# Attention, a dense FFN and routed experts in one kernel: scores and values as two operations of the first stage's plan

## The chip, the cores and the metric

The kernel runs on one core of a Trainium2 chip. The metric is the device time of one execution in microseconds; the kernel before was timed in three runs, and the median counts. The engines have queues of their own and wait for one another through semaphores: TensorE (PE: matmuls; PEld: its weight loads), VectorE (DVE), ScalarE (ACT), GpSimd (POOL) and SyncE (SP). In this kernel SP issues nearly all loads and POOL the stores to scratch memory.

## The reference

Three layers, one behind the other, on 4 batches of 448 tokens (1792 rows of 768):

```python
scores = scale * np.matmul(q, k.transpose(0, 1, 3, 2)) - np.log(S)   # q, k, v: 4 x 12 heads x 448 x 64, f32
attn = 1.0 / (1.0 + np.exp(-scores))                                  # a sigmoid, not a softmax
x = np.matmul(attn, v)                                                # heads are then joined: 1792 x 768
h = x @ w_in                                                          # 768 x 2048, float64 in memory
x = np.maximum(0.01 * h, h) @ w_out                                   # 2048 x 768, float64 in memory
logits = x @ w_gate                                                   # 8 experts, each token goes to one
for e in range(8):
    h = np.maximum(x[mask] @ w1[e], 0.0)
    out[mask] = gate_w[mask, None] * eom[mask, e, None] * (h @ w2[e])
```

Since the sigmoid has no sum over keys, a block of keys is finished by itself: its scores, their sigmoid, and their product with the values, which adds up over the blocks.

## The kernel before

**Stages.** The first stage (`first_batches`, about the first 320 us) does the attention of batches 0 and 1 and most of the dense layer of both. After it the rest runs from generators that take turns (routing, experts, attention of batches 2 and 3). The change is in the first stage alone.

**Attention.** Twelve heads make six pairs, and a pair fills the 128 partitions. Keys and queries are loaded in blocks (`kn`, `qn`: four DMAs each), turned by VectorE (`kt`, `qt`, L1102), rounded by ScalarE to a high part (`kh`, `qh`, L1094), and VectorE makes the low part (`kl`, `ql`, L1098). The 448 keys are four chunks of 112: FRONT is chunks 0 and 1, BACK is 2 and 3. Scores of a chunk are six matmuls (L448: high x high, low x high, high x low, for two heads) into one of two PSUM buffers (`sc`, ring `ps_s`). ScalarE makes the sigmoids (`at`, L455) and so frees the buffer. The values (L461) multiply them with `vn` and add up in the one PSUM buffer `pv` (ring `ps_v`) over the four chunks. When BACK's values are done, ScalarE copies the sum (`x0h` or `x1h`, L1060: the values' copy of the change's name) and VectorE makes its low part (`x0l`, `x1l`, L1064); then `pv` is free again.

**Dense layer.** A weight is needed as a high and a low part (`whi`, L1238, ScalarE; `wlo`, L1242, VectorE), and a product is three matmuls for each block of 128 rows (`mm3`, L369 to L371) into `psm`, which has two buffers. The dense weights lie in memory as 64-bit numbers. Each chunk is loaded in two halves (`r64x`, `r64big`: five buffers, L1183), ScalarE scales one word (`dw`, L1197) and VectorE puts the 32-bit number together by shifts (`raw`, L1202, L1205, L1208); GpSimd stores it to scratch (`wscr`, L1219) for the later batches. An "in" chunk serves 18 matmuls of batch 0 and 18 of batch 1. ScalarE and VectorE make `t`, `g`, `gh` and `gl` out of each finished `psm` (L1280 to L1291).

**What sets the order.** All this is entered in a list of operations (`_Plan`). Each has an engine, a duration, dependencies, buffer rings and a due time, and `order` puts them into one sequence by a simulated clock: the engine that is free first takes the ready operation that is due first. In that order the instructions are emitted, and each engine keeps it. Durations of the plan: two chunks of scores `T_S2` 1.4, the values of two chunks `T_V2` 1.8, a sigmoid 0.9, three dense matmuls 0.6. In `attention_ops`, for each pair and for FRONT and then BACK, one operation on TensorE holds the scores of two chunks and behind them the values of the two chunks before (`both`, L1125): in FRONT those of the preceding pair's BACK (`behind`), in BACK those of this pair's FRONT. The sigmoids depend on that operation:

```python
o = pl.add(PE, T_S2 + (T_V2 if back else 0.0), both, deps=deps, uses=uses, new=new, due=due(cs[1]))
sg[c] = pl.add(ACT, 0.9, sig, deps=(o,), uses=(s_,), new=(at[c],))
```

and so does the values' copy in `finish` (`deps=(last, ...)`, where `last` is `o`), which is entered ahead of them.

Of the kernel before, what the change touches and what calls it, by code (L numbers as in the profile page):

```python
# [118 lines left out]
def kernel(  # L119
# [308 lines left out]
    def turn(a, pool_=ps_t, tag="t"):  # L428
        t = pool_.tile([P, NCH, TP], F32, tag=tag, name="pst")
        for c in range(NCH):  # L430
            nc.tensor.transpose(t[:, c, :], a[:, c].rearrange("p h d -> p (h d)"), ident[:TP, :TP])
        return t.rearrange("p c t -> p (c t)")
# [3 lines left out]
    def stk_tile(nm):  # L436
        return stk_p.tile([P, S], F32R, tag=nm, name=nm)

    def scores(kh, kl, qh, ql, cs):


        sc = []
        for c in cs:
            ks = slice(c * TP, (c + 1) * TP)
            t = ps_s.tile([TP, 2, BANK], F32, tag="s", name="sc")
            for n, (kk, qq) in enumerate(((kh, qh), (kl, qh), (kh, ql))):
                for i, own in enumerate(HALF):
                    nc.tensor.matmul(t[:, i, :S], kk[own, ks], qq[own], start=(n == 0), stop=(n == 2))  # L448
            sc.append(t)
        return sc  # L450

    def squash(sc, a=None):
        if a is None:
            a = at_p.tile([TP, 2, S], F32, tag="at", name="at")
        nc.scalar.activation(a, sc[:, :, :S], ACTF.Sigmoid, bias=nbias[:TP], scale=scale)  # L455
        return a

    def values(pv, vn, at, cs):
        for c in cs:
            for i, own in enumerate(HALF):  # L460
                nc.tensor.matmul(pv[own], vn[:, i, c * D:(c + 1) * D], at[c][:, i], start=(c == 0), stop=(c == NCH - 1))  # L461
# [38 lines left out]
    FRONT, BACK = (0, 1), (2, 3)  # L500
# [504 lines left out]
    def first_batches():  # L1005


        pl = _Plan()
        PE, ACT, DVE, DMA = "PE", "ACT", "DVE", "DMA"
        V = nc.vector  # L1010
        L_QK, L_V, L_W64, L_W, LD_LAT = 1.3, 0.95, 1.55, 1.45, 2.0
        T_A, T_S2, T_V2, T_M = 0.4, 1.4, 1.8, 0.6
# [29 lines left out]
        def load(nm, b, p):  # L1042
            s = pl.slot(nm, 2)
            if (nm, b, p) in nat:
                o = pl.add(DMA, L_QK / 2, lambda: None, new=(s,), due=0.0, lat=LD_LAT)
            else:
                o = pl.add(DMA, L_V if nm == "vn" else L_QK, lambda: load_nat(nm, b, p), new=(s,), lat=LD_LAT)
            nats[nm, b, p] = (s, o)

        def part(back):  # L1050
            pv, vs, vop, b, p, at, sg, cs = back
            if 0 in cs:
                pv.t = ps_v.tile([P, S], F32, tag="v", name="pv")
            values(pv.t, nat["vn", b, p], {c: at[c].t for c in cs}, cs)

        def finish(b, p, pv, last, xs, lows, at):
            def xhi():
                if p == 0:
                    xT[b] = x_tiles(b)
                nc.scalar.copy(xT[b][0][:, p], pv.t)  # L1060

            def xlo():
                xh, xl = xT[b]
                V.tensor_sub(xl[:, p], pv.t, xh[:, p].bitcast(F32))  # L1064

            o = pl.add(ACT, 0.5, xhi, deps=(last, *lows[:1]), uses=(pv, *((xs,) if p else ())), new=() if p else (xs,))
            lows.append(pl.add(DVE, 0.54, xlo, deps=(o,), uses=(pv, xs), due=at + 4.0))

        def attention_ops(b, t0, step):
            for p in range(NP):  # L1070
                for nm in ("kn", "qn", "vn"):
                    load(nm, b, p)
            xs = pl.slot(f"x{b % 2}", 1)
            lows = low_of[b] = []
            behind = None
            for p in range(NP):
                def due(c):
                    return t0 + (p * NCH + c) * step


                stk, ready = {}, []
                for nm in "kq":
                    ns, nop = nats[nm + "n", b, p]
                    own = b >= TURNED
                    ring = (nm, 1) if own else ("m", 2) if b == 0 and nm == "k" else ("t", 1)
                    ts = pl.slot(("turn_" if own else "ps_") + ring[0], ring[1])
                    h, l = stk[nm] = [pl.slot(nm + x, 2) for x in "hl"]

                    def turn_(nm=nm, ts=ts, ring=ring, b=b, p=p):
                        ts.t = turn(nat.pop((nm + "n", b, p)), {"m": ps_m, "t": ps_t}[ring[0]], ring[0])  # L1090

                    def thi(nm=nm, ts=ts, h=h):
                        h.t = stk_tile(nm + "h")
                        nc.scalar.copy(h.t, ts.t)  # L1094

                    def tlo(nm=nm, ts=ts, h=h, l=l):
                        l.t = stk_tile(nm + "l")
                        V.tensor_sub(l.t, ts.t, h.t.bitcast(F32))  # L1098

                    def swing(nm=nm, ts=ts, b=b, p=p):  # L1100
                        ts.t = turn_p.tile([P, S], F32, tag=nm, name=nm + "t")
                        V.transpose(ts.t, nat.pop((nm + "n", b, p)).rearrange("p n d -> p (n d)"))  # L1102

                    o = pl.add(*((DVE, 0.6, swing) if own else (PE, T_A, turn_)), deps=(nop,), uses=(ns,), new=(ts,))
                    o = pl.add(ACT, 0.5, thi, deps=(o,), uses=(ts,), new=(h,))
                    ready += [o, pl.add(DVE, 0.54, tlo, deps=(o,), uses=(ts, h), new=(l,))]
                four = (*stk["k"], *stk["q"])
                pv = pl.slot("ps_v", 1)
                vs, vop = nats["vn", b, p]
                at, sg = {}, {}  # L1110
                for cs in (FRONT, BACK):
                    sc = [pl.slot("ps_s", 2) for _ in cs]
                    new = list(sc)
                    deps, uses = list(ready), list(four)
                    back = behind
                    if cs == BACK:
                        new.append(pv)
                        back = (pv, vs, vop, b, p, at, sg, FRONT)
                    if back:
                        deps += [back[2], *(back[6][c] for c in back[7])]  # L1120
                        uses += [back[1], *(back[5][c] for c in back[7])]
                        if cs == FRONT:
                            uses.append(back[0])

                    def both(cs=cs, sc=sc, four=four, back=back):  # L1125
                        for s_, t in zip(sc, scores(*(x.t for x in four), cs)):
                            s_.t = t
                        if back:
                            part(back)

                    o = pl.add(PE, T_S2 + (T_V2 if back else 0.0), both, deps=deps, uses=uses, new=new, due=due(cs[1]))
                    if back:
                        last = o
                        if cs == FRONT:
                            finish(b, p - 1, back[0], last, xs, lows, due(0))
                    for c, s_ in zip(cs, sc):
                        at[c] = pl.slot("at", 4)

                        def sig(s_=s_, a=at[c]):
                            a.t = squash(s_.t)  # L1140

                        sg[c] = pl.add(ACT, 0.9, sig, deps=(o,), uses=(s_,), new=(at[c],))
                behind = (pv, vs, vop, b, p, at, sg, BACK)

            o = pl.add(PE, T_V2, lambda: part(behind), deps=(behind[2], *(behind[6][c] for c in BACK)),
                       uses=(behind[0], behind[1], *(behind[5][c] for c in BACK)), due=due(NCH) + 2.0)
            finish(b, NP - 1, behind[0], o, xs, lows, due(NCH) + 2.0)
            return xs
# [149 lines left out]
        def summed(b, d, h, jj, lo_ops):  # L1298

            ps = pl.slot("ps_m", 2)  # L1300
            o = None
            for kk in range(HF):
                f = h * HF + kk
                o = product(jj + kk // KQ, kk % KQ, ps, kk == 0, kk == HF - 1, (gs[b, f],), lambda f=f: gs[b, f].t,
                            (lo_ops[kk // KQ], glo[b, f]), o)
            return ps, o
# [41 lines left out]
        for d in range(KD):  # L1348
            lo_ops = [chunk(j + i) for i in range(HF // KQ)]
            ps, o = summed(0, d, 1, j, lo_ops)  # L1350
# [17 lines left out]
            o = pl.add(DVE, 0.62, total, deps=(o, kept), uses=(ps, slot), due=end + 1.0)  # L1368
            o = pl.add(ACT, 0.42, xhi, deps=(o, *((before,) if before else ())), uses=(slot, *((x2,) if d else ())), new=() if d else (x2,), due=end + 1.5)
# [141 lines left out]
```

## Time and profile before

| | us |
|---|---|
| median of 3 runs | 920.3 (918.23 to 921.06) |
| profiled execution | 921.62 |
| its span | 919.9 |
| TensorE matmul busy | 885.1 (96%) |
| TensorE weight load busy | 735.0 (80%) |
| VectorE busy | 510.3 (55%) |
| ScalarE busy | 415.8 (45%) |
| GpSimd busy | 61.0 (7%) |

Busy time is a share of the whole span. In the first 128 us the profile's slices show TensorE with gaps and with a granted clock below full; from there to the end of the stage it shows none. Start times are microseconds from the start of the span. A bracket behind an instruction tells how long its engine stood idle before it and which instruction ended that.

### The profile page before, as it was taken

The numbers are of one execution on the slowest core, as the hardware profiler recorded it, in microseconds if no ns is written. First come the engines' busy times: TensorE is split into PE (matmuls) and PEld (weight loads), VectorE is DVE, ScalarE is ACT, GpSimd is POOL, SyncE is SP. The second block draws the span as 40 slices with busy tenths as digits, with TensorE's granted clock in tenths as the row PEclk, the third lists the DMA queues.
The fourth block names the chain that finished last, engine by engine and source line by source line (L and its number), as shares of the span: only waits on it lengthen the run. The fifth ranks groups of instructions, "written<-read, shape, count | busy, mean of one in ns | idle before, by whom it ended". The sixth has DMA issues, their size and how long they took to land.

```text
span 919.9 us, 13152 instructions
## 1 busy us (share of the span) xinstructions
PE 885.1 (96%) x4544; PEld 735.0 (80%) x4544; DVE 510.3 (55%) x1062; ACT 415.8 (45%) x701; POOL 61.0 (7%) x100
## 2 busy tenths in 40 slices
PE   7879889999999999999999999999999999999996
PEld 4335369999999998977868888777989999799885
DVE  4337646665767887745534746432386433775343
ACT  4567655444444433346453656543345333233331
POOL 2000000011000002210000000000002100120000
PEclk9899999999999999999999999999999999999998
DMA  8569924458433556879535934232455334458433
GB/s 124 92 138 242 281 64 112 127 175 258 151 114 118 164 110 126 165 106 191 118 81 131 230 82 101 67 102 62 133 119 133 98 112 133 77 116 179 125 90 67
DMA packets 294341, 119.97 MB, mean 130 GB/s; under 512 B 206136, under 2 KB 279896, under 8 KB 294272
## 3 DMA queue, kind: packets, MB, share of 16 engines
q1 hardware_dynamic: 286816, 105.87, 49.5%
q0 software_dynamic: 4672, 12.89, 3.9%
q8 instruction: 37, 0.61, 0.3%
q10 hardware_dynamic: 2784, 0.34, 0.3%
q14 instruction: 32, 0.26, 0.1%
HBM read 95.33 MB, written 23.77 MB: 129 GB/s over the span
## 4 chain that ended last, share of the span: by engine, by line
PE 74%; issue 7%; DVE 4%; DMA 2%; ACT 1%; SPq 1%; POOL 0%; POOLq 0%; DVEq 0%; ACTq 0%
PE psm L369 21%; PE psm L371 21%; PE psm L370 21%; PE pv L461 5%; PE sc L448 4%; DMA raw<-in_moe_w_dram 2%; DVE wlo L308 1%; DVE x2t L619 1%; SPq L562 1%; DVE xf L612 1%; PE lgT L571 1%; PE lgT L572 1%; DMA r64big<-in_moe_w_in_dram 1%; DVE gl L552 0%; DVE g L549 0%
## 5 line engine op out<-in xcount | busy, mean ns | idle before, releaser
L371 PE MATMUL psm<-gh,wlo 128*128 128x448 f32 x528 | 191.7, 363 | 0.9 <-DVE wlo L308 0.8
L369 PE MATMUL psm<-gh,whi 128*128 128x448 f32 x528 | 192.4, 364 | 0.0
L370 PE MATMUL psm<-gl,whi 128*128 128x448 f32 x528 | 190.9, 362 | 0.0
L308 DVE TENSOR_TENSOR wlo<-raw,whi 128x512 fp32r<-128x512 f32 (+1 forms) x170 | 132.9, 785 | 77.2 <-ACT whi L300 76.9
L300 ACT CAST whi<-raw 128x512 fp32r<-128x512 f32 (+1 forms) x170 | 118.5, 699 | 94.8 <-PE psm L370 60.1
L369 PE MATMUL psm<-x1h,whi 128*128 128x448 f32 (+1 forms) x288 | 106.3, 369 | 4.7 <-ACT x1h L1060 3.1
L370 PE MATMUL psm<-x1l,whi 128*128 128x448 f32 (+1 forms) x288 | 105.5, 366 | 1.8 <-DVE x1l L1064 1.8
L369 PEld LDWEIGHTS psm<-gh,whi 128*128 128x128 f32 x528 | 99.0, 188 | 9.7 <-issue 3.0
L371 PEld LDWEIGHTS psm<-gh,wlo 128*128 128x128 f32 x528 | 99.0, 188 | 9.6 <-DVE wlo L308 2.7
L369 PE MATMUL psm<-x0h,whi 128*128 128x448 f32 x288 | 105.9, 368 | 0.0
L371 PE MATMUL psm<-x1h,wlo 128*128 128x448 f32 (+1 forms) x288 | 105.3, 366 | 0.0
L371 PE MATMUL psm<-x0h,wlo 128*128 128x448 f32 x288 | 104.2, 362 | 0.0
L370 PE MATMUL psm<-x0l,whi 128*128 128x448 f32 x288 | 104.2, 362 | 0.0
L370 PEld LDWEIGHTS psm<-gl,whi 128*128 128x128 f32 x528 | 99.0, 187 | 6.5
L455 ACT ACTIVATE at<-sc,nbias 112x896 f32<-112x896 f32 x84 | 80.4, 1006 | 12.5 <-PE sc L448 11.7
L461 PE MATMUL pv<-at,vn 112*64 112x448 f32 x336 | 77.3, 593 | 0.0
L369 PEld LDWEIGHTS psm<-x1h,whi 128*128 128x128 f32 x288 | 54.0, 188 | 13.9 <-ACT x1h L1060 6.2
L369 PEld LDWEIGHTS psm<-x0h,whi 128*128 128x128 f32 x288 | 54.0, 188 | 8.1 <-issue 2.7
L370 PEld LDWEIGHTS psm<-x1l,whi 128*128 128x128 f32 x288 | 54.0, 187 | 7.6 <-DVE x1l L1064 3.1
L371 PEld LDWEIGHTS psm<-x1h,wlo 128*128 128x128 f32 x288 | 54.1, 188 | 4.4
L371 PEld LDWEIGHTS psm<-x0h,wlo 128*128 128x128 f32 x288 | 54.0, 187 | 3.9
L370 PEld LDWEIGHTS psm<-x0l,whi 128*128 128x128 f32 x288 | 54.0, 188 | 3.3
(221 smaller groups left out, 1061.6 us busy)
## 6 DMA issues: line engine op xcount, KB each, us to landing
raw<-wscr SPq DMA_DIRECT2D x60, 256.0 KB, 2.7
raw<-in_moe_w_dram SPq DMA_DIRECT2D x32, 384.0 KB, 4.2
raw<-in_moe_w_dram SPq DMA_DIRECT2D x48, 256.0 KB, 3.3
raw<-wscr SPq DMA_DIRECT2D x32, 384.0 KB, 3.8
r64big<-in_moe_w_in_dram SPq DMA_DIRECT2D x24, 384.0 KB, 5.1
r64big<-in_moe_w_out_dram SPq DMA_DIRECT2D x20, 384.0 KB, 4.3
wscr<-raw POOLq DMA_DIRECT2D x16, 384.0 KB, 5.7
wscr<-raw POOLq DMA_DIRECT2D x24, 256.0 KB, 4.4
```

What stands on the lines that cost most here:

```text
L300: nc.scalar.copy(hi, self.got[i])
L308: nc.vector.tensor_sub(lo, r, hi.bitcast(F32))
L369: nc.tensor.matmul(ps, wh, xh, start=first, stop=False)
L370: nc.tensor.matmul(ps, wh, xl, start=False, stop=False)
L371: nc.tensor.matmul(ps, wl, xh, start=False, stop=last)
L448: nc.tensor.matmul(t[:, i, :S], kk[own, ks], qq[own], start=(n == 0), stop=(n == 2))
L455: nc.scalar.activation(a, sc[:, :, :S], ACTF.Sigmoid, bias=nbias[:TP], scale=scale)
L461: nc.tensor.matmul(pv[own], vn[:, i, c * D:(c + 1) * D], at[c][:, i], start=(c == 0), stop=(c == NCH - 1))
L562: by[j % 2].dma_start(dst[:, f:f + SQ].rearrange("(n t) f -> t n f", t=SQ), v[j * SQ:(j + 1) * SQ])
L571: nc.tensor.matmul(lgT[b], wg_c[:, d], xh[:, d, :S], start=(d == 0), stop=False)
L572: nc.tensor.matmul(lgT[b], wg_c[:, d], xl[:, d, :S], start=False, stop=(d == KD - 1))
L612: nc.vector.tensor_add(xf, xh[:, d, :S].bitcast(F32), xl[:, d, :S].bitcast(F32))
```

## The change

One planned operation on TensorE becomes two: `first` (the scores, `T_S2`) and, where there are values to do, a second one (`T_V2`) that depends on the first, on the load of the values and on their sigmoids. The sigmoids of the new scores depend on `first` alone; the copy in `finish` depends on the second. `pv` is claimed by the values' operation instead of the scores'. Durations, due times, buffers and all other code stay.

```diff
                     sc = [pl.slot("ps_s", 2) for _ in cs]
-                    new = list(sc)
-                    deps, uses = list(ready), list(four)
-                    back = behind
-                    if cs == BACK:
-                        new.append(pv)
-                        back = (pv, vs, vop, b, p, at, sg, FRONT)
-                    if back:
-                        deps += [back[2], *(back[6][c] for c in back[7])]
-                        uses += [back[1], *(back[5][c] for c in back[7])]
-                        if cs == FRONT:
-                            uses.append(back[0])
-
-                    def both(cs=cs, sc=sc, four=four, back=back):
+                    back = behind if cs == FRONT else (pv, vs, vop, b, p, at, sg, FRONT)
+
+                    def first(cs=cs, sc=sc, four=four):
                         for s_, t in zip(sc, scores(*(x.t for x in four), cs)):
                             s_.t = t
-                        if back:
-                            part(back)
-
-                    o = pl.add(PE, T_S2 + (T_V2 if back else 0.0), both, deps=deps, uses=uses, new=new, due=due(cs[1]))
+
+                    o = pl.add(PE, T_S2, first, deps=ready, uses=four, new=sc, due=due(cs[1]))
                     if back:
-                        last = o
+                        last = pl.add(PE, T_V2, lambda back=back: part(back), deps=(o, back[2], *(back[6][c] for c in back[7])),
+                                      uses=(back[1], *(back[5][c] for c in back[7]), *((back[0],) if cs == FRONT else ())),
+                                      new=(pv,) if cs == BACK else (), due=due(cs[1]))
```

Since the plan is computed anew, instructions move on every engine. Three places show how; a number behind a name is that of its buffer.

ScalarE in batch 0, third pair, before: the second pair's values are copied (`x0h` from `pv`) ahead of the third pair's four sigmoids (`at`).

```order
L1060 CAST x0h_338<-pv_367 128x448
L455 ACTIVATE at_414<-sc_378,nbias_120 112x896
L455 ACTIVATE at_422<-sc_385,nbias_120 112x896
L455 ACTIVATE at_443<-sc_424,nbias_120 112x896
L455 ACTIVATE at_445<-sc_431,nbias_120 112x896
L1094 CAST kh_447<-kt_402 128x448
L1094 CAST qh_467<-qt_404 128x448
```

The same place after:

```order
L455 ACTIVATE at_404<-sc_378,nbias_120 112x896
L455 ACTIVATE at_413<-sc_385,nbias_120 112x896
L1060 CAST x0h_342<-pv_367 128x448
L455 ACTIVATE at_443<-sc_416,nbias_120 112x896
L455 ACTIVATE at_445<-sc_423,nbias_120 112x896
L1094 CAST kh_447<-kt_402 128x448
L1094 CAST qh_463<-qt_406 128x448
```

The copy has moved from ahead of the two FRONT sigmoids to behind them; the rest of the pair keeps its order.

TensorE in batch 1, its first pair, before: dense matmuls (`psm`) stand between the BACK values of that pair and the scores around them.

```order
L461 MATMUL pv_737<-at_756,vn_625 64x448 x2
L461 MATMUL pv_737<-at_762,vn_625 64x448 x2
L369 MATMUL psm_752<-x0h_338,whi_745 128x448
L370 MATMUL psm_752<-x0l_339,whi_745 128x448
L371 MATMUL psm_752<-x0h_338,wlo_749 128x448
```

After, the first dense matmuls come in batch 1's fifth pair, behind the last values of its fourth (`pv_940`):

```order
L461 MATMUL pv_940<-at_945,vn_858 64x448 x2
L461 MATMUL pv_940<-at_953,vn_858 64x448 x2
L369 MATMUL psm_997<-x0h_342,whi_976 128x448
L370 MATMUL psm_997<-x0l_343,whi_976 128x448
L371 MATMUL psm_997<-x0h_342,wlo_987 128x448
```

Before, 51 dense matmuls stand ahead of the last values of batch 1, after, 18; the 33 others come behind them. The first 54 of each order have the same products: the first weight chunk for both batches and the second for batch 0.

ScalarE in batch 1's fourth pair, the tenth of all, after: two scalings of raw weights (`dw`) stand among its sigmoids.

```order
L1094 CAST kh_872<-kt_830 128x448
L1094 CAST qh_888<-qt_834 128x448
L1187 ACTIVATE dw_897<-r64x_131 128x384
L455 ACTIVATE at_907<-sc_874,nbias_120 112x896
L455 ACTIVATE at_912<-sc_881,nbias_120 112x896
L1060 CAST x1h_770<-pv_862 128x448
L1187 ACTIVATE dw_897<-r64big_130 128x384
L455 ACTIVATE at_945<-sc_920,nbias_120 112x896
```

These are the first two `dw` of the kernel after. Before, the first two stand ahead of the copy of the sixth pair's values and the sigmoids of the seventh pair, three pairs earlier.

## Rows read from the trace of the kernel before

**Rows 1.** Stretches: busy us of PE, PEld, DVE, ACT, POOL; clock; DMA share; GB/s

```profile
7.57:17.26 9.69, 6.63 (x32) 2.83 (x32) 5.19 (x12) 5.75 (x8) 0.00 (x0) 0.82 0.98 136
17.26:63.72 46.46, 38.57 (x212) 15.93 (x210) 15.41 (x27) 26.09 (x36) 0.00 (x0) 0.89 0.56 105
17.26:127.28 110.02, 92.94 (x505) 43.93 (x503) 53.39 (x104) 68.42 (x100) 4.40 (x8) 0.92 0.71 168
128.00:318.00 190.00, 190.00 (x952) 178.09 (x951) 132.92 (x301) 88.26 (x177) 17.29 (x32) 1.00 0.48 148
```

**Rows 2.** Timeline of TensorE, fourth pair: start, length, instruction, [idle before, who ended it]

```profile
34.93 0.46 PE L448 MATMUL sc<-qh,kh 64*112 64x448 f32 x2
...
36.33 1.72 PE L461 MATMUL pv<-at,vn 112*64 112x448 f32 x8
39.60 0.46 PE L448 MATMUL sc<-qh,kh 64*112 64x448 f32 x2 [1.54 <-ACT at L455]
```

**Rows 3.** Timeline of ScalarE, copies of three pairs and the sigmoids between

```profile
30.07 0.53 ACT L1060 CAST x0h<-pv 128x448 fp32r<-128x448 f32 x1 [4.32 <-PE pv L461]
...
38.10 0.53 ACT L1060 CAST x0h<-pv 128x448 fp32r<-128x448 f32 x1 [2.73 <-PE pv L461]
38.53 3.04 ACT L455 ACTIVATE at<-sc,nbias 112x896 f32<-112x896 f32 x3
...
47.72 0.53 ACT L1060 CAST x0h<-pv 128x448 fp32r<-128x448 f32 x1 [3.83 <-PE pv L461]
```

**Rows 4.** Waits from 0 to 240 us: us in total, times, longest

```profile
PE sc L448 <- ACT at L455: 13.7, 8, 3.0
```

**Rows 5.** Timeline of TensorE: a pair without a gap, and the second weight chunk

```profile
111.30 0.46 PE L448 MATMUL sc<-qh,kh 64*112 64x448 f32 x2
...
112.71 1.72 PE L461 MATMUL pv<-at,vn 112*64 112x448 f32 x8
114.36 0.45 PE L448 MATMUL sc<-qh,kh 64*112 64x448 f32 x2
...
127.28 0.47 PE L369 MATMUL psm<-x1h,whi 128*128 128x448 f32 x1 [1.29 <-DVE g L1284]
```

**Rows 6.** TensorE's values: timeline, durations (ns min/median/max), and the mean

```profile
31.56 0.46 PE L448 MATMUL sc<-qh,kh 64*112 64x448 f32 x2 [1.54 <-ACT at L455]
...
33.27 1.72 PE L461 MATMUL pv<-at,vn 112*64 112x448 f32 x8
...
41.80 2.81 PE L461 MATMUL pv<-at,vn 112*64 112x448 f32 x8
L461 PE MATMUL pv<-at,vn x192: 539/539/1008, 14.5 to 123.5; 112*64 112x448 f32 x192
L461 PE MATMUL pv<-at,vn 112*64 112x448 f32 x192 | 47.9, 630 | 0.0
```

**Rows 7.** SP's queue: issue of a key load; DMA issues: KB each, us to landing

```profile
54.33 1.89 SPq L412 DMA_DIRECT2D kn<-in_k_dram  x4
r64x<-in_moe_w_in_dram SPq DMA_DIRECT2D x8, 384.0 KB, 4.5
```

**Rows 8.** Timeline of ScalarE: a scaling of raw weights that waits for its load

```profile
98.34 0.54 ACT L1197 ACTIVATE dw<-r64big 128x384 f32<-128x384 f32 x1 [1.81 <-DMA r64big<-in_moe_w_in_dram]
```

**Rows 9.** Decoding: GpSimd's first and eighth store, VectorE's idle time, its steps

```profile
69.47 0.61 POOL L1219 DMA_DIRECT2D wscr<-raw  x1 [62.37 <-DVE raw L1202]
...
107.28 0.54 POOL L1219 DMA_DIRECT2D wscr<-raw  x1 [2.12 <-DVE raw L1208]
118.10 0.62 DVE L1064 TENSOR_TENSOR x1l<-pv,x1h 128x448 fp32r<-128x448 f32 x1 [7.45 <-ACT x1h L1060]
126.61 1.15 DVE L1284 TENSOR_TENSOR g<-t,psm 128x448 f32<-128x448 f32 x2 [1.35 <-ACT t L1280]
221.17 0.63 DVE L1202 TENSOR_SCALAR raw<-dw 128x384 uint32<-128x384 uint32 x2
...
223.69 0.96 DVE L1242 TENSOR_TENSOR wlo<-raw,whi 128x768 fp32r<-128x768 f32 x1
```

## The prediction, made before the result was known

> **What bounds the kernel now.** I read the stretches first. From 17.26 us, where the second head pair starts, to 127.28 us TensorE is busy 92.94 of 110.02 us; from 128 to 318 us it is busy without a break, 952 matmuls in 190 us or 0.20 us each [rows 1]. So a change to the order of the first stage can win time only ahead of 127.28, and everything behind moves as a block, provided that TensorE stays fed there.
>
> The timeline of one pair comes second, with "front" for key chunks 0 and 1 and "back" for 2 and 3. The front scores of the fourth pair start on TensorE at 34.93 and the values of the pair before at 36.33 [rows 2]. ScalarE stands still for 2.73 us until those values end, copies them at 38.10, and only then, at 38.53, starts the sigmoids of scores that were finished long before [rows 3]. The back scores need the buffer that the first sigmoid frees, so TensorE waits 1.54 us for it and goes on at 39.60 [rows 2]. The next copy starts at 47.72: this pair took 9.62 us, the one before, from the copy at 30.07, 8.03 [rows 3]. The list of waits puts 13.7 us of TensorE's idle time, in 8 waits, on that sigmoid [rows 4].
>
> **The change part by part.** No arithmetic goes or comes. One planned operation (scores, then the values behind them) becomes two. On TensorE the order of batch 0 stays, but for the last values of its sixth pair, which move behind the next scores. On ScalarE the copy of the values moves behind the two front sigmoids, in every pair. The plan is also computed anew: decoding of the dense weights starts near the tenth pair, not the seventh, and TensorE has 18 dense matmuls in the attention of batch 1, not 51.
>
> The floor of the new order is TensorE alone. Two score blocks take 1.41 us (111.30 to 112.71) and a half of the values 1.65 us (112.71 to 114.36) [rows 5]. From 17.26 to 127.28 the kernel before does 22 such double blocks, 23 halves of values and 54 dense matmuls (the row at 127.28 is the 55th [rows 5]). That is 22 x 1.41 + 23 x 1.65 + 54 x 0.20 = 31.0 + 38.0 + 10.8 = 79.8 us. Against 110.0 us, 30.2 us can be won at most: 17.1 us are idle, and 13.1 us are matmuls that run slowly or apart.
>
> Does ScalarE fit under that floor? A pair needs 4 sigmoids (three take 3.04 us [rows 3], so four about 4.0), two casts of about 0.5 each and the copy, 0.43 to the next start [rows 3]: 5.4 us against 6.1 on TensorE. In order, from the start of a pair: front scores done at 0.9 us and 1.5, their sigmoids to 2.8, the values of the pair before end at 3.1, the copy to 3.6, the first back scores done at 3.9, sigmoids to 5.9, casts to 6.8; the next first sigmoid is wanted at 7.0. It fits by some tenths, and TensorE sets the pace: 6.1 us a pair. Four terms come back on top.
>
> Term 1, the start. The second pair's query cast moves ahead of the first sigmoid, and its loads move ahead of the first value load. I take +0.5 us (bounds -1 and +1, one sigmoid either way).
>
> Term 2, decode in ScalarE's queue. The first scaling of raw weights (dw, from r64x) stands ahead of the tenth pair's first sigmoid. Its load is issued behind a key load of 1.89 us of issue time, which waits for a transpose that VectorE does in the ninth pair; a raw load lands 4.5 us after issue [rows 7]. By that the data come some 2.3 us after ScalarE does. Queued behind it are the pair's four sigmoids and two casts, and TensorE waits for those. In the kernel before, such a wait was 1.81 us [rows 8]. I take +2.4; bounds 0 and 5 (two such waits with the gaps that they leave).
> [...]
>
> Term 3, a dense stage with less in stock. Before, eight chunks were decoded and stored by 107.28 (from 69.47 on 5.4 us each), and VectorE then stood 7.45 us idle; now about four are. VectorE decodes a chunk in 2.52 us (221.17 to 223.69), makes its low part in 0.96, and needs 1.15 for two g [rows 9] and as much for two gl: 5.8 of the 7.2 us in which TensorE uses a chunk (36 x 0.20). It can catch up, but for some 18 us its list is full, and a late load is passed on. I take +2.0; bounds 0 and 6 (three late landings of about 2 us).
>
> Term 4, loads and clock. A key load or a query load takes SP 1.89 us to issue [rows 7], about 4 us a pair, under 6.1. The engines of the DMA are 98% busy at 136 GB/s from 7.57 to 17.26 [rows 1]; a pair's 688 kB at that rate take 5.1 us. The loads keep up, with little to spare around the third and fourth pair. The granted clock is 0.82 there and 0.89 up to 63.72 [rows 1]: after the gap of 1.54 us before 39.60 [rows 2] the values at 41.80 take 2.81 us, after the same gap before 31.56 those at 33.27 take 1.72 [rows 6]. [...] With the gaps gone I expect nearly all of that back and take +1.8 for loads and clock; bounds 0 and 8.
> [...]
>
> The sum: 79.8 + 0.5 + 2.4 + 2.0 + 1.8 = 86.5 us where there were 110.0, a gain of 23.5. The profiled execution took 921.62 us, its span 919.9; it lies 1.3 above the median of 920.3. Its span becomes 896.4, the median 896.8: 897. All bounds at their best: 920.3 - 31.2 = 889; all at their worst: 920.3 - 10.2 = 910.
>
> **Rivals.** The clock falls anyway (13 in 100). For it: the pause after the first pair's scores stays. Against: no gap is left in the cycle of a pair. [...]
>
> The loads set the pace (8 in 100). For it: 98% at the start. Against: 0.56 from 17.26 to 63.72 [rows 1]. At 7.2 us a pair, 11 pairs cost 11 x 1.1 = 12 us more: 909.
>
> The edit only moves the wait (7 in 100): sigmoid, score buffer and scores stay in series, and a pair takes the 8.03 us of the quick one [rows 3]. For it: there are two score buffers only. Against: the schedule above. Batch 0's five pairs take 40.2 us, not 46.5; batch 1 takes 6 x 8.03 + 10.8 = 59.0, not 63.6: a gain of 10.9, 909.
>
> Slower: the dense stage starves (4 in 100). The place is VectorE's decode behind the last values, with half the stock. The price is what each of the 16 "in" chunks takes beyond 7.2 us. Without term 3 the gain is 25.5, so it decides from 7.2 + 25.5 / 16 = 8.8 us a chunk; at 9.1 the time is 920.3 - 25.5 + 16 x 1.9 = 925. For it: the stock. Against: 5.4 us a chunk with attention running beside it, and 5.8 us of VectorE [rows 9].
>
> **How the numbers follow.** The forecast has 65 in 100; 3 remain for a time near 920 by something that I haven't seen. The range from 889 to 910 holds the forecast and the first three rivals and leaves out starving. This kernel's measurement tells 0.3%, 2.8 us, from no change: faster 0.93, same 0.03, slower 0.04.
>
> **What would show it.** Right: TensorE's waits for a sigmoid are nearly gone; the seventh pair's scores start near 48 us, not 63.72; a front sigmoid starts about 0.9 us after its scores did, while the values run; the granted clock is near 1.00 from 20 to 60 us; the last values end near 94 us and 54 dense matmuls are done near 101; the lead there is still the same at the end. Term 2 shows as a wait of ScalarE for r64x near 67 us, term 3 as waits of TensorE for g or wlo between 94 and 125 us. Wrong: pairs of 7 us and more in batch 0, or gaps behind 101 us that add up to more than 6 us.

## The result and the profile after

The changed kernel takes 895.84 us, the median of 4 runs (893.94 to 898.74), beside 920.68 for the kernel before in the same session: a ratio of 0.9734, 95% interval 0.9698 to 0.9771. The profiled execution after took 895.02 us, its span 893.4; before it was 921.62 and 919.9.

The stretches come first, as in [rows 1]: busy us of PE, PEld, DVE, ACT and POOL, then the granted clock of TensorE (1.00 is full speed), the DMA share and GB/s.

```profile
0.00:17.18 17.18, 11.58 (x60) 8.27 (x61) 8.41 (x20) 8.44 (x12) 5.65 (x19) 0.90 0.91 132
17.18:63.72 46.54, 46.54 (x308) 22.48 (x308) 22.05 (x39) 39.29 (x53) 0.00 (x0) 1.00 0.69 119
17.18:100.03 82.85, 81.21 (x504) 42.55 (x503) 50.45 (x95) 67.35 (x97) 2.78 (x5) 1.00 0.81 182
100.03:290.70 190.67, 190.67 (x955) 178.89 (x954) 136.71 (x313) 90.58 (x181) 18.89 (x35) 1.00 0.54 165
```

TensorE stands still for 1.64 us in the whole stretch that took 110.02 us before, its clock is 1.00, and the work behind runs without a break as it did. ScalarE shows why (compare [rows 3]):

```profile
28.24 1.00 ACT L455 ACTIVATE at<-sc,nbias 112x896 f32<-112x896 f32 x1
29.13 0.56 ACT L1094 CAST kh<-kt 128x448 fp32r<-128x448 f32 x1
29.58 0.58 ACT L1094 CAST qh<-qt 128x448 fp32r<-128x448 f32 x1
30.40 1.90 ACT L455 ACTIVATE at<-sc,nbias 112x896 f32<-112x896 f32 x2 [0.24 <-PE sc L448]
32.61 0.53 ACT L1060 CAST x0h<-pv 128x448 fp32r<-128x448 f32 x1 [0.31 <-PE pv L461]
33.46 1.91 ACT L455 ACTIVATE at<-sc,nbias 112x896 f32<-112x896 f32 x2 [0.32 <-PE sc L448]
```

The front sigmoids (30.40) now stand ahead of the copy (32.61), and ScalarE waits three times a pair, 0.87 us in all. The front scores of this pair started on TensorE at 29.44, the sigmoid 0.96 us later. A pair takes 6.13 us. One pair still has a gap, the tenth. TensorE first, ScalarE after it:

```profile
66.20 0.46 PE L448 MATMUL sc<-qh,kh 64*112 64x448 f32 x2
...
70.74 0.46 PE L448 MATMUL sc<-qh,kh 64*112 64x448 f32 x2 [1.41 <-ACT at L455]
...
72.72 1.72 PE L461 MATMUL pv<-at,vn 112*64 112x448 f32 x8 [0.20 <-DVE x1l L1064]
74.37 0.46 PE L448 MATMUL sc<-qh,kh 64*112 64x448 f32 x2
```

```profile
69.25 0.55 ACT L1187 ACTIVATE dw<-r64x 128x384 f32<-128x384 f32 x1 [2.32 <-DMA r64x<-in_moe_w_in_dram]
69.69 1.89 ACT L455 ACTIVATE at<-sc,nbias 112x896 f32<-112x896 f32 x2
```

It took 8.17 us, 2.04 more than the others: ScalarE's queue stood 2.32 us at the first decode, the sigmoids behind it. The waits from 0 to 240 us have shrunk from the 13.7 us of [rows 4] (there, too, 3.0 us were a wait of the start-up, at 12.32; the second of the two now is one as well):

```profile
PE sc L448 <- ACT at L455: 3.0, 2, 1.6
```

The last values start at 91.07, and the first dense matmul behind them follows without a gap, so does the 55th:

```profile
92.72 0.47 PE L369 MATMUL psm<-x1h,whi 128*128 128x448 f32 x1
...
100.03 0.36 PE L369 MATMUL psm<-x1h,whi 128*128 128x448 f32 x1
```

Before, the 55th stood at 127.28 [rows 5]: 27.25 us won. The gate's first weight load (lgT) is a landmark behind the first stage. It stood at 318.60 before and stands at 291.24 now, 27.4 earlier; the spans differ by 26.5. The 0.9 between are one wait in the expert stage, where ScalarE stood 1.72 us behind a raw load (386.93):

```profile
388.51 0.46 PE L448 MATMUL sc<-qh,kh 64*112 64x448 f32 x2 [0.96 <-ACT at L455]
```

### The profile page after: what moved, and what is told of

Same layout as the page of the kernel before. It is cut to its first block, busy times and chain, and to the rows that moved or that the text cites. A ratio compares the mean times of both kernels' runs of the same rounds, so it can differ in the third digit from the quotient of the medians.

```text
span 893.4 us, 13151 instructions
## 1 busy us (share of the span) xinstructions
PE 872.4 (98%) x4544; PEld 734.2 (82%) x4544; DVE 510.7 (57%) x1062; ACT 417.2 (47%) x701; POOL 60.9 (7%) x100
## 4 chain that ended last, share of the span: by engine, by line
PE 83%; issue 7%; DVE 4%; SPq 2%; DMA 2%; ACT 1%; POOL 0%; POOLq 0%; DVEq 0%; ACTq 0%
PE psm L369 22%; PE psm L371 22%; PE psm L370 22%; PE pv L461 8%; PE sc L448 7%; SPq L412 2%; DVE wlo L308 1%; DMA qn<-in_q_dram 1%; ACT at L455 1%; DVE x2t L619 1%; DVE xf L612 1%; PE lgT L571 1%; PE lgT L572 1%; DMA raw<-in_moe_w_dram 1%; DMA out_dram<-yt 0%
## 5 line engine op out<-in xcount | busy, mean ns | idle before, releaser
L461 PE MATMUL pv<-at,vn 112*64 112x448 f32 x336 | 71.1, 551 | 0.2 <-DVE x1l L1064 0.2
```

## The experiments

The theory: the place of the copy in ScalarE's queue made the gap, the gap cost its own length and, beside it, clock; with the copy behind the sigmoids TensorE alone sets the pace. The rivals: it is the new plan that wins (decode and dense work elsewhere); or the engines still take turns, so that ScalarE's work shows in full. Each ratio is to the kernel before, run on the same chip; an interval that holds 1 tells no difference. The cuts of code below leave out the lines that only collect the operations to be moved (`trios`, `halves`) or set up a tile. A half is the values of two chunks, a dense piece a group of dense matmuls among the attention's.

| kernel | median us | ratio, 95% interval |
|---|---|---|
| old plan, queue order new | 912.55 | 0.9899 (0.9856 to 0.9942) |
| new plan, queue order old | 918.15 | 0.9955 (0.9934 to 0.9977) |
| old, gaps filled | 923.13 | 1.0013 (0.9992 to 1.0034) |
| new, more ScalarE work | 896.03 | 0.9722 (0.9682 to 0.9763) |
| new, again | 895.11 | 0.9720 (0.9695 to 0.9746) |
| new, first raw load earlier | 893.68 | 0.9701 (0.9673 to 0.9729) |
| old plan, queue order new, 3 loads earlier | 909.23 | 0.9874 (0.9848 to 0.9899) |
| new, all raw loads planned earlier | 898.03 | 0.9748 (0.9722 to 0.9775) |
| old, gaps of batch 0 filled | 919.69 | 0.9981 (0.9961 to 1.0002) |
| the same, 3 loads earlier | 917.05 | 0.9959 (0.9937 to 0.9982) |

**Old plan, queue order new.** The finished order of the kernel before, with each copy and its low part behind the two sigmoids (the last copy of a batch, which no pair of that batch follows, stays):

```
-        for op in pl.order():
+        line = pl.order()
+        for copy, low, *sig in trios:
+            for op in (copy, low):
+                line.remove(op)
+            at_ = max(line.index(op) for op in sig) + 1
+            line[at_:at_] = [copy, low]
+        for op in line:
```

> The kernel before with its own plan (scores and values still one operation, so decode, loads and dense stage stand where they stood); only in the finished order the copy of the values to x0h/x1h, and the low part behind it, are moved behind the two sigmoids of the next pair. Theory (the place of the copy in ScalarE's queue is the whole gain): the 1.5 us gap of TensorE ahead of each pair's second scores goes, the pair falls from 8.0 to about 6.1 us, granted clock 1.00 between 20 and 60, about 897 us; some 1 to 5 us later than the changed kernel if the decode of the old plan then comes too late for a pair. Rival (the new plan is needed, since the double operation was given its start with the copy done, and decode and loads were laid out for a pair of 8 us): the pair stays at 7.5 us or more, 912 us or above.

Neither holds whole: the time is the rival's, the pair is at first the theory's. Up to 50 us the front scores start at 24.47, 30.59, 36.70 and 42.83, 6.12 us a pair, no gap. Then the old plan's decode stands in the queue, three pairs earlier than in the new plan. ScalarE first:

```profile
49.10 0.58 ACT L1097 CAST qh<-qt 128x448 fp32r<-128x448 f32 x1
53.08 0.54 ACT L1206 ACTIVATE dw<-r64x 128x384 f32<-128x384 f32 x1 [3.40 <-DMA r64x<-in_moe_w_in_dram]
...
54.63 0.52 ACT L1061 CAST x0h<-pv 128x448 fp32r<-128x448 f32 x1
```

```profile
56.10 0.72 PE L448 MATMUL sc<-qh,kh 64*112 64x448 f32 x2 [4.17 <-ACT at L455]
...
90.19 0.72 PE L369 MATMUL psm<-x1h,whi 128*128 128x448 f32 x1 [3.49 <-ACT x1h L1061]
```

The faster pace runs ahead of the loads (4.17 us), and the dense pieces that the old plan puts between the pairs wait for the very copy that was moved back (3.49 us; in ScalarE's queue a decode ahead of it waits 2.33 us for its load, at 87.38). About 8 of 25 us remain.

**New plan, queue order old.** The changed kernel, with the two sigmoids put back behind the copy (again inside a batch):

```
+        for copy, low, *sig in trios:
+            for op in sig:
+                line.remove(op)
+            at_ = line.index(copy) + 1
+            line[at_:at_] = sig
```

> The changed kernel with its new plan; only in the finished order the two sigmoids of the next pair are moved back behind the copy of the values, in front of which they now stand. Theory (place in the queue): the gap of TensorE ahead of the second scores is back, 1.4 to 1.6 us in each of the 11 later pairs, and some of the values run at the lower clock again, 912 to 921 us. Rival (the new plan moves decode and loads, and that is the gain): under 900 us.

The time is as the theory had it, and the gap is back, eight times with 1.54 us (not in all 11 pairs); ScalarE's row shows the old order:

```profile
30.47 0.53 ACT L1061 CAST x0h<-pv 128x448 fp32r<-128x448 f32 x1 [4.22 <-PE pv L461]
30.90 3.94 ACT L455 ACTIVATE at<-sc,nbias 112x896 f32<-112x896 f32 x4
```

Ten runs lie between 912.3 and 918.5; the profiled one is the lowest. Time and granted clock go together in them: 912.3 and 913.6 us at a mean of 0.989 and 0.990, the other eight 916.6 to 918.5 at 0.984 to 0.986. So one part alone wins some 8 us, the other some 3, both together 25: the order takes the gap away, and the plan begins the decode three pairs later and moves 33 dense matmuls behind the attention. What of its share each of the two has is not shown.

**New, more ScalarE work.**

```
                         nc.scalar.copy(h.t, ts.t)
+                        nc.scalar.copy(junk, ts.t)
```

> The changed kernel with a second copy of the keys and of the queries of each pair on ScalarE, into a tile that nobody reads: 2 x 0.5 = 1.0 us more ScalarE per pair, with 0.87 us idle in a pair of 6.13 us. Theory (TensorE sets the pace and ScalarE works beside it): pair 6.1 to 6.3 us, at most 3 us slower than the changed kernel, 895 to 899 us. Rival (the two still take turns, ScalarE's work shows in full): pair 7.1 us, 11 us slower, 906 us or more.

TensorE sets the pace. Two more copies a pair, each moving the next start by 0.47 us, fill ScalarE's 0.87 us of slack; the pairs from 25.34 to 68.50 take 6.17 us each and the total rises by 0.2 to 0.9 us:

```profile
43.42 0.56 ACT L1095 CAST kh<-kt 128x448 fp32r<-128x448 f32 x1
43.87 0.58 ACT L1096 CAST junk<-kt 128x448 bf16<-128x448 f32 x1
44.34 0.57 ACT L1095 CAST qh<-qt 128x448 fp32r<-128x448 f32 x1
44.80 0.57 ACT L1096 CAST junk<-qt 128x448 bf16<-128x448 f32 x1
45.27 1.91 ACT L456 ACTIVATE at<-sc,nbias 112x896 f32<-112x896 f32 x2
```

**New, again,** the run beside the next three.

> The changed kernel once more, beside the next three on the same chip: 894 to 899 us by every theory.

It took 895.11 us; its tenth pair shows the same stall (ScalarE 1.89 us at r64x, TensorE 0.99) and takes 7.75 us, 1.62 more than the others.

**New, first raw load earlier.** The load of r64x moves ahead of one load of keys and one of values:

```
+        head = halves[:1]
+        loads = [op for op in line if op.eng == DMA and op.dur]
+        spot = loads[loads.index(head[0]) - 2]
+        for op in head:
+            line.remove(op)
+        spot = line.index(spot)
+        line[spot:spot] = head
```

> The changed kernel; only the first load of raw expert weights (r64x) is issued earlier on SP's queue, ahead of one load of keys and one of values, some 4 us sooner. Theory (the one remaining stall of the stretch, 2.0 us in the tenth pair, is ScalarE's decode that waits 2.32 us for this load): wait and stall go, every pair before the dense stage takes 6.13 us or what its own dense work adds, 2 us faster than the changed kernel, 892 to 896 us. Rival (the stall only moves to the next load, or the load takes bandwidth from the keys): same time or up to 2 us slower, 896 to 899 us.

1.4 us faster than the changed kernel, with no overlap of the runs (892.19 to 894.24 beside 894.25 to 896.96). It is the fastest version of this study. The load goes out at 61.26 (64.55 in the first profile of the changed kernel, 65.52 in the second), and the decode finds its data:

```profile
67.02 0.58 ACT L1095 CAST qh<-qt 128x448 fp32r<-128x448 f32 x1
67.49 0.57 ACT L1188 ACTIVATE dw<-r64x 128x384 f32<-128x384 f32 x1
67.95 1.90 ACT L455 ACTIVATE at<-sc,nbias 112x896 f32<-112x896 f32 x2
```

The back scores of that pair start at 69.93, 3.07 us behind the front ones. The stall was this load.

**Old plan, queue order new, three loads earlier.** The same edit, with `halves[:3]` and three loads passed, on the first experiment's kernel.

> The kernel with the old plan and the copy moved behind the sigmoids; in addition the first three loads of raw weights are issued earlier, ahead of one load each of keys, values and queries, some 5 us sooner. It had held 6.12 us a pair up to 50 us and then lost 17 us against the changed kernel, first where the decode in ScalarE's queue waits 3.40 us for r64x and TensorE 4.17 us behind it. Theory A (the loads of the old plan come too late for the faster pace): this wait goes, about 4 us are won, 907 to 910 us, and what is left are later waits of the same kind. Theory B (the old plan's order of decode, copies and dense pieces among the scores costs it, whatever the loads): less than 2 us won, 911 us or above.

3.3 us won, within A's range. The two runs come from different chips; beside the kernel before on the same chip, the median falls by 13.2 us here and fell by 8.3 there, so the win may be nearer 5. The wait of 4.17 us is 0.55 now, and the fourth load, the first that was not moved, is late instead:

```profile
57.15 0.58 ACT L1098 CAST qh<-qt 128x448 fp32r<-128x448 f32 x1
61.18 0.56 ACT L1207 ACTIVATE dw<-r64big 128x384 f32<-128x384 f32 x1 [3.46 <-DMA r64big<-in_moe_w_in_dram]
```

The 14 us to the changed kernel are not loads alone. From 63.72 to 127 us TensorE is idle for 9.4 us here and for 1.2 in the changed kernel's second run. Five waits of dense pieces for x1h add up to 6.4 us (the first begins at 63.26); these are the two longest:

```profile
86.03 0.47 PE L369 MATMUL psm<-x1h,whi 128*128 128x448 f32 x1 [2.55 <-ACT x1h L1062]
...
95.98 0.47 PE L369 MATMUL psm<-x1h,whi 128*128 128x448 f32 x1 [1.86 <-ACT x1h L1062]
```

Late loads have a part in them: from 54 to 127 us ScalarE still waits 5.7 us for r64big, in three waits.

**New, all raw loads planned earlier.**

```
-        LEAD, EVERY = 16.0, 5.0
+        LEAD, EVERY = 24.0, 5.0
```

> The changed kernel with the planner's LEAD 24 in place of 16: all raw loads, and with them the decode, are planned 8 us, more than a pair, earlier. Theory (only the one late load costs, and ScalarE has room for decode among the pairs): up to 2 us faster, 893 to 896 us. Rival (decode among the pairs takes ScalarE's 0.87 us of slack in a pair and delays the sigmoids, as in the old plan): slower, 897 to 905 us.

Slower by 2.9 us, though not for the rival's reason. The decode moves ahead together with the loads, r64x is in time, and the next load isn't. TensorE then waits 2.08 us (0.99 at the stall of the changed kernel's second run), and the values behind it take 2.33 us:

```profile
68.27 0.54 ACT L1187 ACTIVATE dw<-r64big 128x384 f32<-128x384 f32 x1 [3.15 <-DMA r64big<-in_moe_w_in_dram]
```

**Old, gaps filled.** Three matmuls whose result nobody reads, ahead of the second scores:

```
+                        if cs == BACK:
+                            cold = ps_t.tile([P, P], F32, tag="t", name="cold")
+                            for _ in range(3):
+                                nc.tensor.matmul(cold, ident, ident, start=True, stop=True)
```

> The kernel before with three matmuls of 128x128 f32 on constants, whose result nobody reads, ahead of each pair's second scores, where TensorE waits 1.5 us; the wait on the copy stays. Theory (the gap also costs clock: by the values' two durations some 7 us of the loss are low clock): the granted clock of 20 to 60 rises to about 1.00, the values all take 1.72 us, and the time falls by 4 to 7 us, to 914 to 917 us, although the wait is as long as before. Rival (the clock falls for another reason, or the matmuls stand behind the wait): no change, or up to 5 us slower, 920 to 926 us.

The total is the rival's. The clock did what the theory says: this is the stretch before the decode, first in the kernel before, then here, and the filled gap.

```profile
17.00:54.00 37.00, 30.69 (x162) 12.46 (x160) 12.54 (x23) 21.05 (x29) 0.00 (x0) 0.87 0.54 94
```

```profile
17.00:54.00 37.00, 33.46 (x212) 16.43 (x210) 13.81 (x25) 23.84 (x33) 0.00 (x0) 1.00 0.62 108
```

```profile
33.07 1.72 PE L461 MATMUL pv<-at,vn 112*64 112x448 f32 x8
34.73 0.94 PE L1129 MATMUL cold<-ident 128*128 128x128 f32 x6
36.34 0.46 PE L448 MATMUL sc<-qh,kh 64*112 64x448 f32 x2 [0.68 <-ACT at L455]
```

All values up to 54 us take 1.72 us, and the four pairs from the second to the fifth take 32.1 us (15.63 to 47.69) where they took 36.9 (17.26 to 54.11): 4.8 us for the clock alone, since from the start of a half to the back scores behind it 3.27 us pass in both (36.33 to 39.60 before, 33.07 to 36.34 here). The run gives it back from 55 us on; its landmark stands at 319.99, 1.4 later than before. Two candidates: the fillers of pairs without a gap, and the raw load, for which ScalarE waits 2.43 us at 58.58. The last two runs take them away one by one.

**Old, gaps of batch 0 filled** (`if cs == BACK and b == 0`), **and the same with three loads earlier.**

> The kernel before with the three unread matmuls of 128x128 f32 ahead of the second scores in the seven pairs of the first batch alone (in the earlier run they stood in all eleven to twelve pairs, held the clock up to 54 us, reached the seventh pair 6.4 us earlier than before, and the run still took 923 us). Theory (the clock term is real, and the fillers of the later pairs, which have no gap to fill, gave it back): 2 to 5 us faster than before, 915 to 919 us, with about 2 us of the win lost on the first raw load. Rival (what the early pairs gain is lost again behind loads that come no earlier): 920 us or more.

> The run before with, in addition, the first three loads of raw weights issued ahead of one load each of keys, values and queries. Theory (only the late load swallows what the clock gives): the win shows nearly in full, 914 to 917 us, at least 2 us less than without the earlier loads. Rival (the mixed stretch after 55 us takes as long as it takes): same as without.

The first expectation miscounts: batch 0 has six pairs, and the start reached 6.4 us earlier (47.69 for 54.11) was that of the sixth. The landmark in the two profiles, TensorE's weight load:

```profile
314.60 0.14 PEld L571 LDWEIGHTS lgT<-x0h,wg_c 128*72 128x72 f32 x1
```

```profile
313.28 0.14 PEld L571 LDWEIGHTS lgT<-x0h,wg_c 128*72 128x72 f32 x1
```

Before it stood at 318.60. So without the later fillers 4.0 us are won in the first stage, and 5.3 with the earlier loads as well. In the totals the first is inconclusive (919.69 beside 920.62; its profiled run lost 4.7 us again behind the landmark), the second wins 3.6 us. What the clock cost is real (4.8 us up to 54 us), but the later fillers (5.4 us of the landmark, from 319.99 to 314.60) or late loads (1.3, to 313.28) can hide it.

## Why the prediction held, step by step

Forecast 897 us, measured 895.84: the mechanism and the size were right. Between 17.18 and 100.03 us lie 82.85 us; the sum had 86.5. That the medians lie as near as 1.2 us is partly luck: the span was forecast at 896.4 and measured at 893.4, but the profiled execution before lay 1.3 us above the median that the sum started from, and the one after 0.8 below its own.

- **The floor, 79.8.** It holds, with 0.85 us left out. A dense piece of three between values and scores takes 0.82 us (90.25 to 91.07), not 0.60; the 18 stand in pieces of 6, 6, 3 and 3.
- **ScalarE fits.** 5.4 us a pair beside 6.1 was said; 0.87 us of idle time in 6.13 was found, and the run with 0.9 us more work closed it almost without cost. The rival by which the wait only moves (8.03 us a pair) falls.
- **Term 1, +0.5.** 17.18 in place of 17.26, so -0.1; in the second profile of the changed kernel 18.16, so +0.9 (there the first pair's values took 2.99 us, in the first profile 2.06). Within the bounds.
- **Term 2, +2.4.** 2.04 us, at the place, the load and the pair that were named. Issuing that load earlier gives 1.4 back, in a session in which the stall cost 1.62. ScalarE kept the order of its queue there: the sigmoid that follows the late decode, at 69.69, was for scores that TensorE had begun at 66.20.
- **Term 3, +2.0, and term 4, +1.8.** These two were sized too high; both measured nothing. TensorE has no gap from 92.72 on to the expert stage: VectorE's 5.8 us a chunk (an estimate from [rows 9]) in 7.2 were enough even with half the stock. No run shows the 1.8 us of term 4: the clock is 1.00 from 17.18 to 290.70, and the loads kept up at a DMA share of 0.69 up to 63.72 and 0.81 up to 100.03. What came back of the clock shows in the matmuls of the values: 186 of them were busy for 45.18 us before, from 17.26 to 127.28, and for 39.73 us now, from 17.18 to 100.03. The rivals of the clock, the loads and the starving dense stage fall with them.
- **The signs.** The seventh pair's scores start at 47.82 (near 48 was said), the last values end at 92.72 (94), the 55th dense matmul stands at 100.03 (101). Of the 27.25 us won there 26.5 are left at the end.

The sum that was measured: 79.8 + 0.85 + 2.04 = 82.7, where the 2.04 include the wait of 0.20 for x1l at 72.72. The 0.16 that are missing to 82.85 are what the round figures of the floor leave out (the 36 dense matmuls from 92.72 on take 7.31 us, not 7.2).

What the prediction didn't price is the plan. It counted 18 dense matmuls in the attention instead of 51 and took the gain as that of the order in the queue. The runs show that the order alone would have given 8 of the 25 us; that loss was not among the rivals. The list that it read 13.7 us from has three more rows of that stretch, 6.2 us of idle time, and all of them are waits of dense pieces; in the changed kernel they are gone:

```profile
PE psm L369 <- ACT x1h L1060: 3.1, 4, 1.2
PE psm L370 <- DVE x1l L1064: 1.8, 4, 1.2
...
PE psm L369 <- DVE g L1284: 1.3, 1, 1.3
```

Of the 14 us that are left when the first loads come in time, some 8 are more idle time of TensorE from 63.72 to 127 us. No run moved the dense pieces alone, so the share of decode and of dense pieces in the rest stays open.

What the low clock cost the kernel before was taken out by itself for the first part only: 4.8 us up to 54 us, by filling the gaps. The values of the whole stretch were busy 5.5 us longer than in the changed kernel (45.18 beside 39.73); no run takes out the rest alone.

## What to carry to other kernels

ScalarE kept to its queue here: a decode waited 2.32 us for its load, and the sigmoids of scores begun at 66.20 came behind it, at 69.69. In such a queue an instruction that waits for something late belongs behind the work whose inputs are ready; two operations tied into one in a plan can be what puts it ahead. When the pace goes up, look at what was laid out for the old pace: here decode, loads and dense pieces became the next wait, and the same reordering under the old plan was worth a third. A single load that landed too late for ScalarE cost its wait downstream, 2.04 us of that pair on TensorE: moving that one load won 1.4 us, planning all of them earlier lost 2.9.

## What was not expected of the hardware

- Gaps of the same length did not always bring the low clock. With the new plan and the old queue order gaps of 1.54 us stand ahead of 31.96, 39.96 and 47.97, and yet the seven halves from 28.70 to 52.73 all take 1.72 us in the profiled run, such as this one:

```profile
31.96 0.46 PE L448 MATMUL sc<-qh,kh 64*112 64x448 f32 x2 [1.54 <-ACT at L455]
...
33.64 1.72 PE L461 MATMUL pv<-at,vn 112*64 112x448 f32 x8
```

  In the kernel before, three of the eleven halves from 18.67 to 63.72 (at 23.66, 41.80 and 50.92) took 2.81 to 3.25. Behind two longer waits of the first experiment, 4.17 and 3.49 us, matmuls ran slowly each time: five rows of scores took 0.58 us each from 56.62 on, where five ahead of the wait had taken 0.36 to 0.38 (50.76 to 51.56), and three took 0.57 from 92.40 on, the one at 93.79 again 0.36.
- Gaps of 0.68 us between fillers and scores left the granted clock at 1.00 up to 54 us.
- TensorE's busy time over the run fell from before by 12.7 us, to 872.4, with the same arithmetic: busy time contains the clock (the same eight matmuls of a half count 1.72 or 2.81 us).
